# Even frequencies of a split DFT: two quarter-size units in place of two half-size units (FNet mixing and gated convolution FFN, one core)

## The chip, the cores and the metric

The kernel runs on one core of a Trainium2 chip. The metric is the device time of one execution in microseconds (us). A core has five engines that run side by side: PE (TensorE, matmuls; its weight loads are listed as PEld), DVE (VectorE), ACT (ScalarE), POOL (GpSimd) and SP, which issues most DMAs. SBUF is the working memory; matmuls write to PSUM, which holds banks of 512 fp32 numbers in each of 128 partitions.

## The reference

```
X = np.fft.fft(x, axis=1)                 # x: (8, 3136, 256), over the sequence
X = np.fft.fft(X, axis=2)                 # over the features
x1 = X.real
h = np.maximum(x1 @ w_in, 0.0)            # w_in: (256, 1024)
conv_out = sum over k of conv_w[k] * (h shifted by k - 1 rows)    # 3 taps, zero padded
out = (h * sigmoid(conv_out)) @ w_out     # w_out: (1024, 256)
```

All of it is fp32. A matmul in fp32 stands in the trace as two records, each with a weight load of its own.

## The kernel before, in words

**Sequence DFT by halves.** The DFT over 3136 rows is taken of folded data: rows n, S-n, S/2-n and so on are added or subtracted on DVE (`fold_ops`), so that a quarter of the rows (784) stays, in tiles `w` of 98 or 99 partitions, for even and for odd frequencies apart. For one batch and one of the two sums, `sn` = 0 (cosine, tile `pt`) or 1 (sine, tile `qt`), the values at the frequencies k = 0 to 1568 are made by products of these tiles with tables of cosines and sines (`product`, line 273; `table`, line 216). The sum over n goes over four groups q = 0 to 3 (n mod 4 decides the group; 98 or 99 rows each).

A split halves the columns: with the groups q = 3 and 1 summed to a number a, and q = 2 and 0 to a number b, frequency k is a + b, and its mirror image M - k is a - b (or b - a for the sine). So a product is made only for half of the frequencies, and one addition and one subtraction give the rest.

- **Odd k** (`odd_even`, line 308, and `odd`, line 323) are made with one more level of it. `odd_even` makes the groups q = 1 and q = 3 for 196 columns each; ACT copies one half to a tile `as`, and DVE's addition and subtraction (lines 318 and 320) put 392 numbers into another tile `as`. `odd` then makes the groups 0 and 2 for 392 columns, and DVE combines the `as` tile with them into `pt` or `qt` at every second place (lines 330 and 332).
- **Even k** (`even(sn, c)`, line 286) are made by two units, one for c = 0 and one for c = 1: the frequencies 0, 4, 8, ... (197 columns) and 2, 6, 10, ... (196 columns). Each unit has four matmuls of 197 or 196 columns: q = 3 and 1 accumulate in the first part of a PSUM bank, q = 2 and 0 in the part behind it. The columns of the table are read with a step of 2, the PSUM output is contiguous. ACT copies the first part to `as` (line 295), then DVE adds and subtracts straight into `pt` or `qt` at every fourth place (lines 299 and 302).

**Order of the work.** The rest of the kernel goes in 256 steps (8 batches x 4 chunks of the sequence x 8 groups of 128 features of d_ff). In cycle t of the loop PE runs `products` of step t+1 (matmuls into `pb` and `pa`: the feature DFT merged with `w_in`), `mm2` of step t-3 (six matmuls `po` with `wout`), and, last, matmuls of a DFT unit, which all write to `pd` (one PSUM bank of a pool with one buffer). DVE runs `combine` (line 692), two taps of the convolution (line 702), one piece of side work between the taps, and its half of the gate (line 723). ACT copies `pb` (683), fills `pa` (662), does the first tap (697), the sigmoid (715) and the copies of the output (742); POOL does the other half of the gate (722, 725) and issues indirect loads of x (131).

The eight units of batch b run during the loop cycles of batch b-1: `cs` (line 857 on) gives each of them n // 8 cycles. For b = 2 to 7 that is four cycles, one matmul in each; for b = 1 it is one or two cycles, four or two matmuls in each, in nine cycles together. A unit's ACT copy and its DVE part (`u.copy` and `u.fin`, lines 861 and 862) stand in the cycle after its last matmul. Batch 0's units run ahead of the loop (line 786), in `po` buffers, with no steps beside them. The first matmul of the next unit waits until the DVE part of the one before has read `pd`.

Of the kernel before, what the change touches and what calls it, by code (L numbers as in the profile page):

```python
# [9 lines left out]
F32 = mybir.dt.float32  # L10
# [3 lines left out]
ALU = mybir.AluOpType  # L14
# [22 lines left out]
def kernel(  # L37
# [10 lines left out]
    nc = tc.nc  # L48
    B, S, D = x.shape
    F = moe_w_in.shape[1]  # L50
    P = 128
    M = S // 2
    Q4 = S // 4
# [4 lines left out]
    HE = Q4 // 2 + 1  # L58
    HO = Q4 // 2
# [14 lines left out]
    asp = ctx.enter_context(tc.tile_pool(name="asp", bufs=4))  # L74
# [11 lines left out]
    vt = nc.vector.tensor_tensor  # L86
# [4 lines left out]
    def mm(o, l, r, start, stop):  # L91
        nc.tensor.matmul(o, l, r, start=start, stop=stop, skip_group_check=True)  # L92
# [120 lines left out]
    PQ, eb, er = {}, {}, {}  # L213
    ed = edp.tile([B, (RC // 2 + 1) * RC], F32, name="ed")

    def table(k, st, q, cols):
        return tabs[st // 2][0:k, st, q, cols] if st < 2 else tabs[1][0:k, st - 2, q, cols]
# [32 lines left out]
    class Unit:  # L250
# [19 lines left out]
        def fin(self):  # L270
            self.fin_(self.p)

    def product(o, w, st, q, cols, start, stop):

        def f(p):
            k = KR if q == HQ - 1 else NP
            mm(p[o], w(k, q), table(k, st, q, cols), start, stop)
        return f

    def units(b):  # L280
        def w(i):
            return lambda k, q: wt[b][i // 4][0:k, i % 4, q, :]

        a_ = {}

        def even(sn, c):
            n = HO // 2 + 1 - c
            nh = HO // 2
            cols = slice(c, HE, 2)
            mms = [product((slice(0, P), slice(j * n, (j + 1) * n)), w(2 * sn + c), sn, q, cols, q == qs[0], q == qs[1])  # L290
                   for j, qs in enumerate(((3, 1), (2, 0))) for q in qs]

            def copy(p):
                a_[sn, c] = asp.tile([P, HO + 2], F32, name="as", tag="as")
                nc.scalar.copy(out=a_[sn, c][:, 0:n], in_=p[:, 0:n])

            def fin(p):
                a, bb, t = a_[sn, c], p[:, n:2 * n], PQ[b][sn]
                vt(t[:, 2 * c:Q4 + 1:4], a[:, 0:n], bb, op=ALU.add)
                hi = t[:, M - 2 * c:Q4:-4]  # L300
                x0, x1 = (bb[:, 0:nh], a[:, 0:nh]) if sn else (a[:, 0:nh], bb[:, 0:nh])
                vt(hi, x0, x1, op=ALU.subtract)
            return Unit(b, mms, copy, fin)

        def stat(sn):
            return ((w(4 + 2 * sn), 2 + sn), (w(5 + 2 * sn), 4 + sn))

        def odd_even(sn):
            mms = [product((slice(0, P), slice(j * QO, (j + 1) * QO)), wf, st, q, slice(0, QO), i == 0, i == 1)
                   for j, q in ((1, 1), (0, 3)) for i, (wf, st) in enumerate(stat(sn))]  # L310

            def copy(p):
                a_[sn], a_["e0"] = [asp.tile([P, HO + 2], F32, name="as", tag="as") for _ in range(2)]
                nc.scalar.copy(out=a_["e0"][:, 0:QO], in_=p[:, 0:QO])

            def fin(p):
                a, e0, e2 = a_[sn], a_["e0"][:, 0:QO], p[:, QO:2 * QO]
                vt(a[:, 0:QO], e0, e2, op=ALU.add)
                x0, x1 = (e2, e0) if sn else (e0, e2)
                vt(a[:, HO - 1:QO - 1:-1], x0, x1, op=ALU.subtract)  # L320
            return Unit(b, mms, copy, fin)

        def odd(sn):
            prods = [(q, wf, st) for q in (0, 2) for wf, st in stat(sn)]
            mms = [product((slice(0, P), slice(0, HO)), wf, st, q, slice(0, HO), i == 0, i == 3)
                   for i, (q, wf, st) in enumerate(prods)]

            def fin(p):
                a, bb, t = a_[sn][:, 0:HO], p[:, 0:HO], PQ[b][sn]
                vt(t[:, 1:Q4 + 1:2], a, bb, op=ALU.add)  # L330
                x0, x1 = (bb, a) if sn else (a, bb)
                vt(t[:, M - 1:Q4:-2], x0, x1, op=ALU.subtract)
            return Unit(b, mms, lambda p: None, fin)

        def feature():

            mms = []
            for i in range(2):
                for j, qs in enumerate(((3, 1), (2, 0))):
                    for c in range(2):  # L340
                        n = HO // 2 + 1 - c
                        o = 32 * (2 * j + c)
                        mms.append(product((slice(o, o + 1), slice(0, n)),
                                           lambda k, q, c=c: ea[b][0:k, c, q:q + 1], 0, qs[i],
                                           slice(c, HE, 2), i == 0, i == 1))

            def copy(p):
                a_["e"] = [asp.tile([P, HO + 2], F32, name="as", tag="as") for _ in range(2)]
                for j in range(2):
                    for c in range(2):  # L350
                        n = HO // 2 + 1 - c
                        o = 32 * (2 * j + c)
                        nc.scalar.copy(out=a_["e"][c][0:1, j * n:(j + 1) * n], in_=p[o:o + 1, 0:n])

            def fin(p):
                t = er[b]
                nh = HO // 2
                for c in range(2):
                    n = nh + 1 - c
                    a, bb = a_["e"][c][0:1, 0:n], a_["e"][c][0:1, n:2 * n]  # L360
                    gt(t[:, 2 * c:Q4 + 1:4], a, bb, op=ALU.add)
                    gt(t[:, M - 2 * c:Q4:-4], a[:, 0:nh], bb[:, 0:nh], op=ALU.subtract)
            return Unit(b, mms, copy, fin, True)

        def begin():
            PQ[b] = [pqp.tile([P, NK], F32, name=nm, tag=nm) for nm in ("pt", "qt")]

        def row():
            er[b] = erp.tile([1, NK], F32, name="er", tag="er")
            nc.sync.dma_start(out=er[b], in_=PQ[b][1][P - 1:P, :])  # L370

        def flip():

            act(er[b][:, 3:NK:4], er[b][:, 3:NK:4], AF.Copy, scale=-1.0)

        def store():
            nc.sync.dma_start(out=ed[b:b + 1, 0:NK], in_=er[b])

        return (begin, [odd_even(1), odd(1), even(1, 0), even(1, 1), feature(), odd_even(0), odd(0),
                        even(0, 0), even(0, 1)], row, flip, store)  # L380

    class Feature:

# [368 lines left out]
    def keep_on(banks):  # L752

        for p in banks:
            mm(p.rearrange("p (s q d) -> p s q d", s=2, q=2), wt[0][1][0:NP, 1, 0], wt[0][1][0:NP, 0:2, 0:2],
               True, True)

    begin, us, row, flip, store = units(0)
    begin()

# [34 lines left out]
    n = chunks[0].k1  # L795
    p = psd.tile([P, 512], F32, name="pd", tag="pd")
# [54 lines left out]
    for b in range(1, B):  # L851
        begin, us, *_ = units(b)
        us = us[0:4] + us[5:]
        c0, n = ends[b], per * b - 3 - ends[b]
        at(max(c0, per * (b - 1) + 1), "pe", begin)
        cs = [c0 + i * n // len(us) for i in range(len(us) + 1)]
        for i, u in enumerate(us):
            k = cs[i + 1] - cs[i]
            for j in range(k):
                at(cs[i] + j, "pe", lambda u=u, j=j, k=k: u.matmuls(j, k))  # L860
            at(cs[i + 1], "act", u.copy)
            at(cs[i + 1], "dve", u.fin)
            if b > 1:
                taken.add(cs[i + 1])
        at(cs[-1] - 2, "load", lambda b=b: spread(b, range(len(chunks) - 1)))
        at(per * b + 1, "load", lambda b=b: spread(b, [len(chunks) - 1]))
    for b in range(1, B):
        ops, singles = fold_ops(b)
        c0, n = ends[b - 1], ends[b] - ends[b - 1]
# [14 lines left out]
    n = len(steps)  # L884
# [101 lines left out]
```

## Time and profile before

| | |
|---|---|
| median of three runs | 1202.16 us (1201.81 to 1203.91) |
| the profiled execution's own time | 1202.16 us |
| span of that execution, from its first to its last instruction | 1200.4 us |
| units of batch 0 for even k on PE | 34.28 to 40.09 us |
| units of batch 1 on PE | 149.7 to about 196 us |
| units of batches 2 to 7 on PE | from 233 to about 1049 us |
| granted TensorE clock, mean | 0.997 |

Busy time of an engine counts the time in which at least one of its instructions was in flight. In the views by line a group stands as: line, engine, operation, output tile <- input tiles, shapes, count, then busy time and mean ns of one instruction, then idle time ahead of it and what ended it. A timeline line gives start, length, engine, line, operation, tiles, shapes (for matmuls rows*columns of the weights, then partitions x columns that stream) and count; matmuls overlap, so what one costs is the distance from its start to the next start, not its length. The chain of waits follows the work that ended last back from the end.

### The profile page before, as it was taken

What the parts mean: (1) busy time and instruction counts of PE and PEld (TensorE: products, weight loads), DVE (VectorE), ACT (ScalarE), POOL (GpSimd) and SP (SyncE); (2) the same over time, 40 slices, a digit from 0 to 9 for tenths busy, and PEclk for the clock granted to TensorE, in tenths of its full rate; (3) what the DMA queues carried; (4) which work ended last, traced back from release to release, by engine and by line L of the source; (5) the groups of instructions that cost most, each with busy time, mean ns of one, the idle gap of its engine ahead of it and who ended that gap; (6) DMA issues with size and microseconds to landing.
All of it is one profiled execution on the core that took longest, in us unless ns stands there. A gap on an engine that the chain in (4) does not pass through costs nothing.

```text
span 1200.4 us, 15341 instructions
## 1 busy us (share of the span) xinstructions
PE 1162.4 (97%) x4802; PEld 895.6 (75%) x4802; DVE 1130.0 (94%) x1642; ACT 883.4 (74%) x1840; POOL 474.2 (40%) x540
## 2 busy tenths in 40 slices
PE   4978999999999999999999999999999999999998
PEld 2756677677777777777777777777777777777776
DVE  7899999999999999999999999999998988899996
ACT  2667656777677777777777777787776777788884
POOL 5325636464263432624345243632334223342224
PEclk9999999999999999999999999999999999999999
DMA  9712243212031210202021020310000100110000
GB/s 230 187 34 81 58 53 101 62 54 74 8 95 45 67 40 30 79 27 81 26 89 51 17 64 27 95 40 27 27 27 28 32 27 27 47 34 27 27 28 31
DMA packets 70068, 66.08 MB, mean 55 GB/s; under 512 B 28107, under 2 KB 57683, under 8 KB 69987
## 3 DMA queue, kind: packets, MB, share of 16 engines
q1 hardware_dynamic: 64349, 51.98, 15.3%
q0 software_dynamic: 5120, 12.85, 3.5%
q8 instruction: 38, 0.62, 0.2%
q14 instruction: 43, 0.35, 0.1%
q10 hardware_dynamic: 518, 0.28, 0.1%
HBM read 39.33 MB, written 25.74 MB: 54 GB/s over the span
## 4 chain that ended last, share of the span: by engine, by line
PE 83%; DVE 7%; issue 4%; POOL 3%; ACT 2%; DMA 1%; ACTq 0%; POOLq 0%; DVEq 0%; SPq 0%
PE po L92 50%; PE pb L92 13%; PE pa L92 12%; PE pd L92 8%; DVE g L702 3%; POOL xh L131 1%; DVE h L692 1%; DVE g L723 1%; DMA xh<-in_x_dram 1%; ACT nb L683 1%; ACT g L715 0%; POOL left L725 0%; ACT os L742 0%; POOL g L722 0%; DVE w L194 0%
## 5 line engine op out<-in xcount | busy, mean ns | idle before, releaser
L92 PE MATMUL po<-wout,g 128*128 128x256 f32 x3072 | 708.6, 380 | 15.9 <-DVE g L723 15.7
L92 PEld LDWEIGHTS po<-wout,g 128*128 128x128 f32 x3072 | 581.5, 190 | 163.8 <-DVE g L723 30.4
L702 DVE SCALAR_TENSOR_TENSOR g<-h,cw,g 128x770 f32<-128x770 f32 (+1 forms) x512 | 573.1, 1119 | 6.0 <-ACT g L697 2.1
L722 POOL TENSOR_TENSOR g<-g,h 128x385 f32<-128x385 f32 (+1 forms) x256 | 271.5, 1061 | 681.3 <-ACT g L715 482.6
L683 ACT ACTIVATE nb<-pb 128x386 f32<-128x386 f32 (+3 forms) x512 | 227.2, 498 | 168.2 <-PE pb L92 167.6
L715 ACT ACTIVATE g<-g 128x385 f32<-128x385 f32 (+2 forms) x512 | 244.4, 529 | 101.4 <-DVE g L702 99.6
L692 DVE CUSTOM_DVE_ANT_0 h<-pa,nb 128x386 f32<-128x386 f32 (+3 forms) x512 | 264.3, 556 | 6.5 <-POOL h L668 6.5
L697 ACT ACTIVATE g<-h,cw 128x770 f32<-128x770 f32 (+1 forms) x256 | 244.0, 953 | 0.0
L92 PE MATMUL pb<-qt,G 127*128 127x387 f32 (+2 forms) x512 | 212.7, 496 | 1.4 <-ACT G L631 1.0
L92 PE MATMUL pa<-pt,G 128*128 128x387 f32 (+2 forms) x512 | 211.8, 494 | 0.0
L662 ACT ACTIVATE pa<-eb,ge 128x387 f32<-128x387 f32 (+2 forms) x256 | 154.5, 604 | 2.7 <-DVE h L692 1.9
L92 PEld LDWEIGHTS pa<-pt,G 128*128 128x128 f32 x512 | 96.8, 189 | 73.6 <-issue 18.2
L723 DVE TENSOR_TENSOR g<-g,h 128x385 f32<-128x385 f32 (+1 forms) x256 | 146.4, 572 | 2.2 <-ACT g L715 2.2
L92 PE MATMUL pd<-tab,w 98*128 98x196 f32 (+3 forms) x448 | 126.7, 374 | 0.0
L131 POOL DMA_INDIRECT xh<-in_x_dram,idx x64 | 107.6, 1681 | 13.3 <-issue 10.6
L92 PEld LDWEIGHTS pb<-qt,G 127*128 127x128 f32 x512 | 93.9, 190 | 19.5 <-issue 1.6
L92 PEld LDWEIGHTS pd<-tab,w 98*128 98x128 f32 (+1 forms) x448 | 84.7, 191 | 12.3
L725 POOL TENSOR_TENSOR left<-g,h 128x64 f32<-128x64 f32 x64 | 64.8, 1012 | 0.0
L742 ACT COPY os<-po 128x256 f32<-128x256 f32 x196 | 57.5, 390 | 8.0 <-PE po L92 4.7
L156 DVE TENSOR_TENSOR xh<-xh 98x1020 f32<-98x1020 f32 (+1 forms) x32 | 39.5, 1239 | 2.3 <-DMA xh<-in_x_dram,idx 2.3
L167 DVE TENSOR_TENSOR xh<-xh 98x1024 f32<-98x1024 f32 (+1 forms) x32 | 38.9, 1217 | 0.1
L193 DVE TENSOR_TENSOR w<-xh 98x508 f32<-98x508 f32 (+1 forms) x32 | 22.8, 714 | 0.2
(114 smaller groups left out, 324.9 us busy)
## 6 DMA issues: line engine op xcount, KB each, us to landing
out_dram<-os SPq DMA_DIRECT2D x192, 128.0 KB
xh<-in_x_dram SPq DMA_DIRECT2D x16, 784.0 KB
eb<-ed SPq DMA_DIRECT2D x16, 193.5 KB
tab<-dft_seq_dram SPq DMA_DIRECT2D x4, 589.5 KB
raw<-in_moe_w_in_dram SPq DMA_DIRECT2D x4, 512.0 KB
raw<-in_moe_w_out_dram SPq DMA_DIRECT2D x1, 2048.0 KB
eb<-ed SPq DMA_DIRECT2D x8, 209.0 KB
eb<-ed SPq DMA_DIRECT2D x7, 193.0 KB
```

The costliest lines, as they stand in the source:

```text
L92: nc.tensor.matmul(o, l, r, start=start, stop=stop, skip_group_check=True)
L131: nc.gpsimd.indirect_dma_start(out=xh[b, h][0:NP, 7 - m].rearrange("p q d -> p (q d)"), out_offset=None, in_=bass.AP(tensor=x.tensor, offs ...
L662: act(pa[s][:, 0:n], eb[b, c], AF.Copy, scale=ge[:, f:f + 1])
L683: act(nb[s][:, i, cols], p[:, cols], AF.Copy, scale=-1.0 if i else 1.0)
L692: nc.vector._custom_dve(TENSOR_ADD_SAT, out=to, in0=a[:, cols], in1=c[:, i, cols], s0=BIG, s1=0.0)
L697: act(gs[s], hs[s][:, 0:n], AF.Copy, scale=cw[:, 0, s[2]:s[2] + 1])
L702: stt(out=g, in0=h[:, k:k + n], scalar=cw[:, k, f:f + 1], in1=g, op0=ALU.mult, op1=ALU.add)
L715: act(gs[s][:, c], gs[s][:, c], AF.Sigmoid)
L722: gt(g[:, p], g[:, p], h[:, p], op=ALU.mult)
L723: vt(g[:, v], g[:, v], h[:, v], op=ALU.mult)
L725: gt(left[:, f, b % 2 * LEFT:(b % 2 + 1) * LEFT], g[:, r], h[:, r], op=ALU.mult)
L742: nc.scalar.copy(out=osb[:, j % 2], in_=pt[:, j % 2])
```

## The change

For even k, the two units by c become two units by q, as for odd k:

- `even_even(sn)` takes q = 3 and 1 for the first n = 197 columns alone. It has four matmuls, each by itself (start and stop), of 99 or 98 columns: c = 0 and c = 1 of q = 3 to the even and odd places of the first part of the bank, c = 0 and c = 1 of q = 1 to those of the second part. ACT copies the first part (197 columns) to an `as` tile, and DVE's addition and subtraction write 197 and 196 numbers contiguously to another `as` tile.
- `even(sn)` takes q = 2 and 0 for all 393 columns: four matmuls, c = 0 (197 columns, to the even places of the bank) and c = 1 (196 columns, to the odd places), two accumulating on each. It has no ACT copy. DVE's addition (393 numbers) and subtraction (392) write to `pt` or `qt` at every second place.

The number of units, of matmuls, of weight loads and of DVE instructions stays; PSUM outputs that were contiguous have a step of 2 now. The number of `as` tiles taken stays as well.

```diff
-        def even(sn, c):
-            n = HO // 2 + 1 - c
-            nh = HO // 2
-            cols = slice(c, HE, 2)
-            mms = [product((slice(0, P), slice(j * n, (j + 1) * n)), w(2 * sn + c), sn, q, cols, q == qs[0], q == qs[1])
-                   for j, qs in enumerate(((3, 1), (2, 0))) for q in qs]
+        def even_even(sn):
+
+            n = HO // 2 + 1
+            mms = [product((slice(0, P), slice(j * n + c, (j + 1) * n, 2)), w(2 * sn + c), sn, q, slice(c, n, 2),
+                           True, True) for j, q in ((0, 3), (1, 1)) for c in range(2)]
 
             def copy(p):
-                a_[sn, c] = asp.tile([P, HO + 2], F32, name="as", tag="as")
-                nc.scalar.copy(out=a_[sn, c][:, 0:n], in_=p[:, 0:n])
+                a_["v", sn], a_["e4"] = [asp.tile([P, HO + 2], F32, name="as", tag="as") for _ in range(2)]
+                nc.scalar.copy(out=a_["e4"][:, 0:n], in_=p[:, 0:n])
 
             def fin(p):
-                a, bb, t = a_[sn, c], p[:, n:2 * n], PQ[b][sn]
-                vt(t[:, 2 * c:Q4 + 1:4], a[:, 0:n], bb, op=ALU.add)
-                hi = t[:, M - 2 * c:Q4:-4]
-                x0, x1 = (bb[:, 0:nh], a[:, 0:nh]) if sn else (a[:, 0:nh], bb[:, 0:nh])
-                vt(hi, x0, x1, op=ALU.subtract)
+                a, e4, e2 = a_["v", sn], a_["e4"], p[:, n:2 * n]
+                vt(a[:, 0:n], e4[:, 0:n], e2, op=ALU.add)
+                x0, x1 = (e2[:, 0:n - 1], e4[:, 0:n - 1])[::1 if sn else -1]
+                vt(a[:, HO:n - 1:-1], x0, x1, op=ALU.subtract)
             return Unit(b, mms, copy, fin)
+
+        def even(sn):
+
+            mms = [product((slice(0, P), slice(c, HE, 2)), w(2 * sn + c), sn, q, slice(c, HE, 2), q == 2, q == 0)
+                   for c in range(2) for q in (2, 0)]
+
+            def fin(p):
+                a, bb, t = a_["v", sn][:, 0:HE], p[:, 0:HE], PQ[b][sn]
+                vt(t[:, 0:Q4 + 1:2], a, bb, op=ALU.add)
+                x0, x1 = (bb, a) if sn else (a, bb)
+                vt(t[:, M:Q4:-2], x0[:, 0:HO], x1[:, 0:HO], op=ALU.subtract)
+            return Unit(b, mms, lambda p: None, fin)
...
-        return (begin, [odd_even(1), odd(1), even(1, 0), even(1, 1), feature(), odd_even(0), odd(0),
-                        even(0, 0), even(0, 1)], row, flip, store)
+        return (begin, [odd_even(1), odd(1), even_even(1), even(1), feature(), odd_even(0), odd(0),
+                        even_even(0), even(0)], row, flip, store)
```

## The prediction

> **What bounds the kernel now.** I read the page first, by engine and by the chain of waits:
>
> ```profile
> PE 1162.4 (97%) x4802; PEld 895.6 (75%) x4802; DVE 1130.0 (94%) x1642; ACT 883.4 (74%) x1840; POOL 474.2 (40%) x540
> PE 83%; DVE 7%; issue 4%; POOL 3%; ACT 2%; DMA 1%; ACTq 0%; POOLq 0%; DVEq 0%; SPq 0%
> ```
>
> PE and DVE both look full, so the share of busy time does not decide; the chain does, and it runs on PE for 83% of the span. Then the busy times of stretches (after each stretch: length, PE, PEld, DVE, ACT, POOL, clock, DMA):
>
> ```profile
> 150.00:200.00 50.00, 50.00 (x210) 38.85 (x210) 48.17 (x76) 32.13 (x66) 22.96 (x23) 1.00 0.44 84
> 240.00:381.00 141.00, 141.00 (x586) 109.98 (x585) 134.38 (x201) 105.57 (x218) 66.14 (x70) 1.00 0.18 58
> 522.00:663.00 141.00, 141.00 (x588) 110.31 (x587) 134.50 (x197) 107.00 (x220) 57.00 (x64) 1.00 0.17 53
> ```
>
> From 240 us on PE is never without a matmul in flight, and all units of batches 2 to 7 lie there or just ahead. That a busy PE also runs at its pace needs start distances, since lengths overlap. The timeline of PE gives them:
>
> ```profile
> 527.87 0.51 PE L92 MATMUL pd<-tab,w 98*128 98x197 f32 x2
> 528.23 0.81 PE L92 MATMUL pb<-qt,G 127*128 127x387 f32 x2
> 528.88 0.82 PE L92 MATMUL pa<-pt,G 128*128 128x387 f32 x2
> 529.53 2.75 PE L92 MATMUL po<-wout,g 128*128 128x256 f32 x12
> 532.12 0.52 PE L92 MATMUL pd<-tab,w 98*128 98x197 f32 x2
> ```
>
> One cycle is 4.25 us: pd 0.36, pb 0.65, pa 0.65, po 2.59. Nothing is left between the pieces. So PE's own work sets the pace here, and a nanosecond taken from `pd` is a nanosecond of the time, as long as DVE, ACT and POOL keep up.
>
> **The change on PE.** Columns first. For one sum of one batch, before: four matmuls of 197 and four of 196, 1572 columns. After: two of 99, two of 98, two of 197, two of 196, 1180. The matmuls and their weight loads stay eight. So the question is what a matmul of 98 or 99 columns costs. The nearest rows, of 197 columns (above), 196 columns read contiguously, and one column, all with weights of 128 columns:
>
> ```profile
> 561.85 0.50 PE L92 MATMUL pd<-tab,w 98*128 98x196 f32 x2
> 562.18 0.81 PE L92 MATMUL pb<-qt,G 127*128 127x387 f32 x2
> ...
> 45.75 0.95 PE L92 MATMUL po<-dm,win 128*128 128x1 f32 x8
> 46.56 0.90 PE L92 MATMUL pb<-qt,G 127*128 127x386 f32 x2
> 47.29 0.81 PE L92 MATMUL pa<-pt,G 128*128 128x386 f32 x2
> ```
>
> 196 columns cost 0.33 us for the pair of records, 197 columns with a step of 2 in the table 0.36 (0.348 to 0.360 over the loop's even units; I use 0.355). One column costs far more than nothing: eight records take 45.75 to 46.56 = 0.81, and the pb behind them takes 0.73 to its pa in place of 0.65, so 0.89 / 8 = 0.111 per record. That is the weight load, which can't be outrun: 0.222 per matmul. By columns alone 99 would cost half of 0.355 = 0.178. The larger one holds: 0.222. A matmul of `even_even` saves 0.355 - 0.222 = 0.133 us; bounds are 0.177 saved (if only columns counted) and a loss of 0.025 (if the load, 0.190 long in its rows, did not overlap at all and set 0.38). I take 0.133, since the one-column row is the same load at the same pace.
>
> `even` keeps matmuls of 197 and 196 columns with the same step in the table: saving 0, if writing to PSUM with a step of 2 costs nothing. No matmul of before writes with a step, so this is the unknown. From below: nothing, since columns, weights and reads are the same (a gain has no source). From above: as if it walked over the skipped columns too, which is a matmul of 392 columns, 0.661 in place of 0.355 (574.54 to 575.20 on the timeline). Between them: reading with the step costs 0.355 against 0.335, 6%; and DVE, writing 196 numbers at every fourth place, takes 0.35 where contiguous ones take 0.28 (chain rows below), 25%. I take 0, as PE's own row with a step is nearest, and even that is nearly free; I keep 0.02 (6%) for my range.
>
> The rule that speaks against the change: the Trainium skill, "PSUM — Partial Sum Buffer", section Specifications, says that PSUM lines hold 8 bytes, two fp32, and that a non-contiguous access pattern slows matmuls significantly. It gives no factor. No run here shows it; if the factor were two (an estimate of mine from "two per line"), `even` would lose what the change gains, and more: the sum would be that of the first rival below. The reason why I do not follow it: an fp32 matmul streams a column in 0.85 ns (0.335 / 2 / 196), and the page does not say at which pace its line rule was seen.
>
> Per batch: 8 matmuls of `even_even` (4 for each sum) x 0.133 = 1.06 us less on PE.
>
> **The change on DVE and ACT.** The chain of waits shows DVE's pace without idle time, ahead of the loop:
>
> ```profile
> 33.57 0.27 DVE as L318
> 33.84 0.28 DVE as L320
> ...
> 34.77 0.47 DVE pt L332
> ...
> 40.92 0.35 DVE qt L299
> 41.27 0.36 DVE qt L302
> ```
>
> Before, four instructions at every fourth place: 4 x 0.35 = 1.42 per sum. After, two like L318 and two like L332: 2 x 0.275 + 2 x 0.48 = 1.51. So DVE gets 0.09 more per sum, 0.18 per batch, of about 134 busy in 141. ACT loses one copy of 0.33 per sum. With it goes a wait: the tile `as` rows give 26.2 us of DVE's idle time in 26 waits to ACT's copies of line 295, 1.0 us each; half of the units had their copy removed, so DVE gets back up to 14 x 1.0 in the loop, against 7 x 0.18 = 1.3 more work. What `even`'s DVE part then waits for is PE itself, whose matmul ended the cycle before; line 330 in the same place waits 0.9 us in 14. DVE stays covered by PE: of a stretch of 141 it had about 6.6 idle.
>
> The `pd` bank is free for the next unit when `even`'s two DVE instructions end: 0.96 in place of 0.71 after their start, which comes up to 1.0 earlier. No new wait.
>
> **Where the gain arrives.** Against the profiled execution (time 1202.16, span 1200.4; its time is also the median):
>
> - Batches 2 to 7: 6 x 1.06 = 6.4. Nothing follows the loop but PE's own end, so it stays.
> - Two places in these batches where PE did wait, 0.3 us each, at 497.9 and 779.9 for DVE's gate, at the end of a run of fold instructions. There up to four faster matmuls (0.5) lie ahead, so PE will wait longer; DVE's removed wait pays part back. I take 0.2 lost at each: -0.4.
> - Batch 1, units at 150 to 196 with PE full; from 187 to 211 the chain goes over ACT and POOL, then DVE. What PE gains until 187 moves that start; DVE-bound stretches may take some. Between 0.5 and 1.06: 0.8.
> - Batch 0: PE saves 1.06, but the chain from 40.07 to 47 is DVE's, which takes 0.18 longer, behind narrowing of weights that ends at 40.15 as before. PE's saving is hidden: -0.2.
>
> Sum: 6.4 - 0.4 + 0.8 - 0.2 = 6.6 us less. 1202.16 - 6.6 = **1195.6 us**. With 6% on each stepped write (8 x 0.02 x 7 = 1.1) and 1 us of the gain lost to waits, 1197.7; with `even_even` at its columns' price (8 x 0.044 x 7 = 2.5 more) 1193.1. Own range of this case: 1193.5 to 1198.
>
> **Rivals.**
>
> 1. *The stepped write sets the pace: slower.* One mechanism, in PE on `even`'s matmuls. At its upper price `even` goes from 0.355 to 0.661, 8 x 0.306 = 2.45 more per batch, and `even_even` to about 0.335, saving 0.02 x 8 = 0.16. Net 2.3 per batch, all on the bounding engine in seven batches: +16, **1218 us**. It decides from where `even` loses what `even_even` gains, 0.133 of 0.355: a stepped column 37% dearer. For it: DVE's stepped write shows that such a price exists. Against it: the stepped read costs PE 6%.
> 2. *Partial price, or a weight load that costs more: no change.* With DVE's 25% as the price, `even` loses 0.09 a matmul, and 8 x (0.133 - 0.09) = 0.35 per batch is left: 2.4 in seven batches, less the 0.6 of waits: **1200.4**. With the load not overlapped, +0.2 per batch: 1203.6.
> 3. *DVE takes over.* If PE's gain turns into waits for DVE's gate in half of the batches, as it did twice before, 3.3 is left: **1198.9**. DVE's removed waits speak against it. It is still faster.
>
> **Chances.** Forecast 0.66; DVE takes over 0.09; no change (2) 0.12; slower (1) 0.13. What a measurement of this kernel can tell from no change is about 0.2%, 2.4 us. Faster by more: 0.66 + 0.09 = 0.75, plus nothing from (2): 0.75. Same 0.12, slower 0.13. The range runs from 1193.5 over (3) to the better part of (2), 1202: it leaves out (1), 0.13, and the tails, 0.06.
>
> **What would show it.** `pd` matmuls of 98 and 99 columns with start distances of 0.11 (0.22 the pair): right; 0.17 or more: weight load mis-sized. `pd` of 197 columns at 0.355: stepped write free; at 0.38 to 0.66: the rivals. The group of line 295's successor with 14 copies in the loop and half the idle time ahead of DVE; PE busy in all of 240 to 1190 as before. Were PE's idle time for the gate to grow beyond 2 us, the third rival is there. The prediction is wrong above all if the stepped write has a price above a third.

## The result and the profile after

The changed kernel takes 1196.78 us (median of 4 runs, 1195.33 to 1197.23), the kernel before 1203.04 (median of 4, 1201.81 to 1204.11) in the same sessions: a ratio of 0.9946, 95% interval 0.9929 to 0.9963. It is faster, by 6.3 us. (Against 1202.16, the median that the forecast started from, it is 5.4.) The profiled execution of the changed kernel has a span of 1195.3 us against 1200.4. From `odd_even` on (the former line 308) the lines of the code are ten higher (L702, L712, L733 are the former L692, L702, L723); `even_even` copies in L294 and combines in L298 and L300, `even` combines in L310 and L312.

The page's lines of engine busy time and of the chain by engine:

```profile
PE 1156.0 (97%) x4802; PEld 888.5 (74%) x4802; DVE 1135.0 (95%) x1642; ACT 878.4 (73%) x1824; POOL 477.5 (40%) x540
PE 86%; DVE 5%; issue 3%; POOL 3%; ACT 2%; DMA 0%; ACTq 0%; POOLq 0%; DVEq 0%; SPq 0%
```

PE lost 6.4 us of busy time, ACT 5.0 with its 16 copies, and the chain lies on PE even more than before. The same stretches as in the prediction:

```profile
150.00:200.00 50.00, 50.00 (x216) 39.07 (x217) 49.19 (x77) 33.95 (x69) 24.05 (x27) 1.00 0.42 82
240.00:381.00 141.00, 141.00 (x589) 109.48 (x589) 136.29 (x203) 106.23 (x218) 68.84 (x70) 1.00 0.19 58
522.00:663.00 141.00, 141.00 (x591) 110.00 (x591) 136.20 (x199) 106.94 (x222) 57.04 (x64) 1.00 0.17 53
```

PE is never without a matmul from 240 us on (before, it had two pauses there, of 0.17 and 0.16), and does more of them in each stretch (591 in place of 588 in the last one). PE's timeline shows at what pace:

```profile
527.22 0.36 PE L92 MATMUL pd<-tab,w 99*128 99x98 f32 x2
527.42 0.84 PE L92 MATMUL pb<-qt,G 127*128 127x387 f32 x2
528.10 0.82 PE L92 MATMUL pa<-pt,G 128*128 128x387 f32 x2
528.75 2.75 PE L92 MATMUL po<-wout,g 128*128 128x256 f32 x12
...
539.59 0.52 PE L92 MATMUL pd<-tab,w 98*128 98x197 f32 x2
539.94 0.81 PE L92 MATMUL pb<-qt,G 127*128 127x387 f32 x2
```

Read the start distances. The pair of 98 columns takes 0.20 to the next start; the pb behind it takes 0.68 to its pa where it took 0.65. The cheaper pair leaves a debt of 0.02: the first record takes 0.093, the second 0.111, which is what a weight load took in the one-column row, and 0.347 in place of 0.328 pass between pb's two records (mean over the 22 places with 387 columns). I read that as loads that run late. Together 0.224, the price of two weight loads. The pair of 197 columns, whose output now has a step of 2, takes 0.354, as it did with a contiguous output.

On DVE's side, the groups by the tiles `as` (durations min/median/max) and the waits for ACT's copies:

```profile
L298 DVE TENSOR_TENSOR as<-as,pd x14: 360/361/362, 167.3 to 1027.7; 128x197 f32<-128x197 f32 x14
L310 DVE TENSOR_TENSOR qt<-as,pd x7: 552/558/569, 172.4 to 973.9; 128x393 f32<-128x393 f32 x7
...
  ACT as L324: 12.5, 10
  ACT as L294: 9.8, 13
```

DVE waits 22.3 us for the copies where it waited 26.2 + 8.5 = 34.7; `even` waits for none.

**Where the time went.** I split the span at the first matmul of `po<-wout,g` (the loop's start) and at the same matmul of batch 7, and take the batch periods between, from the starts in the traces (batches count from 0; the units of batch b run in the period of batch b-1). All runs but one, which adds work behind the loop, in us:

| run | loop start | from there to batch 7 | period of batch 2 | period of batch 3 | median of the runs |
|---|---|---|---|---|---|
| before | 60.84 | 1012.09 | 139.52 | 142.54 | 1202.2 to 1203.0 |
| after | 63.75 | 1004.12 | 138.04 | 141.51 | 1196.78 |
| after_again | 63.06 | 1004.13 | 138.04 | 141.51 | 1196.52 |
| pe_undone | 62.00 | 1011.29 | 139.08 | 142.53 | 1202.71 |
| pe_alone | 64.27 | 1004.89 | 138.48 | 141.49 | 1197.64 |
| old_b0 | 63.18 | 1004.12 | 138.04 | 141.51 | 1195.96 |
| flat_write | 62.40 | 1004.10 | 138.04 | 141.51 | 1196.12 |
| flat_tables | 62.77 | 1003.18 | 137.90 | 141.36 | 1195.18 |
| fill | 61.13 | 1004.31 | 138.04 | 141.51 | 1195.23 |
| before_fill | 61.28 | 1012.10 | 139.51 | 142.53 | 1202.47 |
| fill_flat_tables | 61.51 | 1003.22 | 137.90 | 141.36 | 1194.02 |

The loop gained 7.97 us. The start gave 2.9 of them back in the profiled execution: 7.97 - 2.90 = 5.07, the spans differ by 5.1. Two questions follow: which part of the change carries the loop's gain, and whether the start's loss belongs to the change.

### The profile page after: what moved, and what is told of

The parts are those of the page before. It is cut to its first block, busy times and chain, and to the rows that moved or that the text cites. A ratio compares the mean times of both kernels' runs of the same rounds, so it can differ in the third digit from the quotient of the medians.

```text
span 1195.3 us, 15307 instructions
## 1 busy us (share of the span) xinstructions
PE 1156.0 (97%) x4802; PEld 888.5 (74%) x4802; DVE 1135.0 (95%) x1642; ACT 878.4 (73%) x1824; POOL 477.5 (40%) x540
## 4 chain that ended last, share of the span: by engine, by line
PE 86%; DVE 5%; issue 3%; POOL 3%; ACT 2%; DMA 0%; ACTq 0%; POOLq 0%; DVEq 0%; SPq 0%
PE po L92 53%; PE pb L92 13%; PE pa L92 13%; PE pd L92 7%; DVE g L712 2%; POOL xh L131 1%; DVE h L702 1%; DVE g L733 1%; ACT nb L693 0%; ACT os L752 0%; ACT g L725 0%; POOL left L735 0%; POOL g L732 0%; DVE w L194 0%; ACT pa L672 0%
## 5 line engine op out<-in xcount | busy, mean ns | idle before, releaser
L712 DVE SCALAR_TENSOR_TENSOR g<-h,cw,g 128x770 f32<-128x770 f32 (+1 forms) x512 | 580.1, 1133 | 6.2 <-ACT g L707 2.2
L732 POOL TENSOR_TENSOR g<-g,h 128x385 f32<-128x385 f32 (+1 forms) x256 | 276.2, 1079 | 673.0 <-ACT g L725 471.1
L702 DVE CUSTOM_DVE_ANT_0 h<-pa,nb 128x386 f32<-128x386 f32 (+3 forms) x512 | 264.1, 556 | 7.4 <-POOL h L678 6.5
L733 DVE TENSOR_TENSOR g<-g,h 128x385 f32<-128x385 f32 (+1 forms) x256 | 147.4, 576 | 2.2 <-ACT g L725 2.2
L92 PE MATMUL pd<-tab,w 98*128 98x196 f32 (+3 forms) x448 | 118.4, 356 | 0.0
L92 PEld LDWEIGHTS pb<-qt,G 127*128 127x128 f32 x512 | 91.2, 190 | 19.3 <-ACT G L641 2.0
L178 POOL COPY w<-xh 98x4 f32<-98x4 f32 (+1 forms) x32 | 20.6, 644 | 6.1 <-DVE xh L167 3.6
```

Source lines behind the costliest of these rows:

```text
L702: nc.vector._custom_dve(TENSOR_ADD_SAT, out=to, in0=a[:, cols], in1=c[:, i, cols], s0=BIG, s1=0.0)
L712: stt(out=g, in0=h[:, k:k + n], scalar=cw[:, k, f:f + 1], in1=g, op0=ALU.mult, op1=ALU.add)
L732: gt(g[:, p], g[:, p], h[:, p], op=ALU.mult)
L733: vt(g[:, v], g[:, v], h[:, v], op=ALU.mult)
```

## Experiments

My theory for the loop: PE's own work sets the pace, and PE's saving carries the gain. The rival: the removed ACT copies and their waits carry it. For the start, two theories: DVE's longer units, or PE's clock.

**after_again** is the changed kernel once more, with no edit.

> The changed kernel once more, unaltered. Both theories of the gain: 1196 to 1197.5 us. It tells about the start: in the first profile of the changed kernel the first matmul of the loop with wout began at 63.7 us in place of 60.8. If the change itself delays the start (the two DVE units, 0.4 us longer, let PE run idle), 63 to 64 us again; if the half clock there, at 41.6 to 48.4 us, is chance, about 61 us.

Measured: 1196.52 us (ratio 0.9951, 0.9937 to 0.9964), loop start 63.06. So the late start came again, with half clock at 42.8 to 46.2 us.

**pe_undone** gives `even_even` its old number of columns:

```diff
-            mms = [product((slice(0, P), slice(j * n + c, (j + 1) * n, 2)), w(2 * sn + c), sn, q, slice(c, n, 2),
+            mms = [product((slice(0, P), slice(j * n, (j + 1) * n - c)), w(2 * sn + c), sn, q, slice(c, HE, 2),
```

> The changed kernel with DVE's and ACT's part as changed, but even_even's four matmuls have 197 or 196 columns again (contiguous output, other table columns, so the even frequencies come out as other sums). Theory PE: the loop's batches 1 to 7 lose their 1.04 us each again, 7.2 in all: 1203.5 to 1204.5 us, batch periods at 142.5 in place of 141.5. Rival, the removed ACT copies and their waits carry the gain: the time stays at 1196 to 1198 us.

Measured: 1202.71 us, ratio 1.0000 (0.9991 to 1.0009). The whole gain is gone, and the periods are 1.01 to 1.04 longer than in the changed kernel: PE's columns carry it. But the loop is 0.80 shorter than before (in its profile a later start, 62.00, hides that), by batches 2 and 4, whose periods lost 0.44 each. There DVE was what PE waited for. Before, and then in this run:

```profile
496.87 0.81 PE L92 MATMUL pb<-qt,G 127*128 127x386 f32 x2
497.52 0.81 PE L92 MATMUL pa<-pt,G 128*128 128x386 f32 x2
498.50 0.70 PE L92 MATMUL po<-wout,g 128*128 128x256 f32 x2 [0.17 <-DVE g L723]
```

```profile
497.79 0.50 PE L92 MATMUL pd<-tab,w 99*128 99x196 f32 x2
498.12 0.81 PE L92 MATMUL pb<-qt,G 127*128 127x386 f32 x2
498.77 0.81 PE L92 MATMUL pa<-pt,G 128*128 128x386 f32 x2
499.42 2.75 PE L92 MATMUL po<-wout,g 128*128 128x256 f32 x12
```

pa to po is 0.65 here, a matmul's own time, in place of 0.98 before; the other 0.11 of the 0.44 lies between the first two matmuls of `po`. With DVE's and ACT's part as changed, the wait of PE is gone. Which piece of that part does it (the removed copies, or DVE's other instructions) was not tried apart.

**pe_alone** takes the other half: the kernel before, with the matmuls of `even(sn, 0)` cut, DVE and ACT as they were.

```diff
+            def some(j, i, q):
+                cut = (0, HO // 4 + 1, n)
+                o, e = (cut[i], cut[i + 1]) if c == 0 else (0, n)
+                return product((slice(0, P), slice(j * n + o, j * n + e)), w(2 * sn + c), sn, q,
+                               slice(c + 2 * o, c + 2 * e - 1, 2), i == 0 or c == 0, i == 1 or c == 0)
+            mms = [some(j, i, q) for j, qs in enumerate(((3, 1), (2, 0))) for i, q in enumerate(qs)]
```

> The kernel before, with only PE's saving: the four matmuls of the unit even(sn, 0) have 99 or 98 columns, each alone writes its part of the bank; DVE and ACT as before (so q = 3 and 1 are not summed there and these frequencies come out as other values). No stepped PSUM output. Theory PE: 7 x 1.04 = 7.3 less in the loop, nothing changed ahead of it: 1195.5 to 1197 us, and PE waits at the two places before batch ends (497.9 and 779.9 before) grow from 0.3 to 0.6 us, since DVE is not relieved. Rival (DVE and ACT carry it): 1202 to 1203 us.

Measured: 1197.64 us (0.9961, 0.9947 to 0.9974), with a late start (64.27). The loop is 7.20 shorter than before: 7 x 1.03. The same place in its timeline:

```profile
497.92 0.81 PE L92 MATMUL pa<-pt,G 128*128 128x386 f32 x2
498.90 1.78 PE L92 MATMUL po<-wout,g 128*128 128x256 f32 x7 [0.17 <-DVE g L726]
```

The wait is there, 0.98 from pa to po, and has not grown, as I had expected it to. So the two parts add up: 7.20 from PE, 0.80 from DVE and ACT, 7.97 in the changed kernel.

**old_b0** keeps the kernel before for batch 0, whose units run ahead of the loop.

```diff
+        e1, e0 = [[even_c(s, 0), even_c(s, 1)] if b == 0 else [even_even(s), even(s)] for s in (1, 0)]
+        return (begin, [odd_even(1), odd(1), *e1, feature(), odd_even(0), odd(0), *e0], row, flip, store)
...
```

(`even_c` is `even(sn, c)` of the kernel before.)

> The changed kernel, but batch 0, ahead of the loop, keeps the two units by c of the kernel before; batches 1 to 7 are as changed. If the change delays the start by 2.9 us: 1193.5 to 1194.5 us, loop start at 60.8. If the delay is chance or the clock's: 1196 to 1197 us, within 0.3 of the changed kernel in the same call.

Measured: 1195.96 us (0.9947, 0.9933 to 0.9960), loop start 63.18, with half clock at 43.1 to 46.5. The old units did not bring the early start back, and the half clock came with them too. So DVE's longer units are not needed for a late start; the clock came into question. The stretches 41.6 to 48.4 us (PE, PEld, DVE, ACT, POOL, then the clock) of before and of the first profile after:

```profile
41.60:48.40 6.80, 6.34 (x32) 4.64 (x32) 6.56 (x16) 3.93 (x10) 3.29 (x6) 1.00 0.62 206
```

```profile
41.60:48.40 6.80, 6.34 (x18) 4.64 (x18) 6.46 (x14) 1.90 (x5) 2.83 (x6) 0.50 0.67 212
```

PE is as busy, with 18 matmuls for 32, at a clock of 0.50. PE's timeline there, before and then in the changed kernel:

```profile
40.09 0.91 PE L92 MATMUL pd<-er,one 1*128 1x386 f32 x2
41.02 1.02 PE L92 MATMUL po<-dm,win 128*128 128x1 f32 x8
41.91 1.97 PE L92 MATMUL po<-win,dm 128*128 128x256 f32 x8
44.34 0.92 PE L92 MATMUL pb<-qt,G 127*128 127x386 f32 x2 [0.46 <-issue]
```

```profile
39.66 0.91 PE L92 MATMUL pd<-er,one 1*128 1x386 f32 x2
41.40 1.64 PE L92 MATMUL po<-dm,win 128*128 128x1 f32 x8 [0.82 <-ACT eb L809]
42.90 3.76 PE L92 MATMUL po<-win,dm 128*128 128x256 f32 x8
47.12 1.55 PE L92 MATMUL pb<-qt,G 127*128 127x386 f32 x2 [0.46 <-ACT G L641]
```

PE has finished its shorter units at 39.73, 1 us ahead of DVE, whose narrowing of weights ends at 40.75 (before, both ended at about 40.15). It sits idle for 0.82 between matmuls of one row (`pd<-er,one`) and matmuls of one column (`po<-dm,win`). Then the eight matmuls of `po<-win,dm`, 1.97 long before, take 3.76, and the loop's first products come 2.8 later.

**fill** takes that stretch away: a dense matmul in the gap, and the one-column matmuls (`column(0)`) behind the eight matmuls `po<-win,dm` (`blocks(0)`).

```diff
-    column(0)
+    keep_on([idle])
     for f in load_ops(1, 0, nc.sync):
         f()
     blocks(0)
+    column(0)
```

> The changed kernel with another order of PE at 40 to 48 us: one dense matmul of 512 columns (into the idle bank) where PE sat idle for 1 us behind the product with 'one', and column(0), eight records of one column, behind blocks(0) in place of ahead of it. Theory clock: in the changed kernel PE reaches this place 1 us sooner than DVE and is idle there, 2.6 to 2.9 us of little work in a row, and the clock falls to half for 3.4 to 6.8 us, which delays the loop by 2 to 3 us in most executions. With no such stretch left the clock stays at 1.0 there, the loop starts at 60.5 to 61.5 us, and the median falls to 1193.5 to 1194.5. Rival (the delay is DVE's 0.4 us longer work and late loads): loop start at 63, 1196 to 1197 us.

Measured: 1195.23 us (0.9937, 0.9925 to 0.9950), loop start 61.13, clock 1.0 throughout this part:

```profile
38.80 0.91 PE L92 MATMUL pd<-er,one 1*128 1x386 f32 x2
39.64 1.12 PE L92 MATMUL pb<-w 98*128 98x512 f32 x2
40.60 2.22 PE L92 MATMUL po<-win,dm 128*128 128x256 f32 x8
42.66 0.95 PE L92 MATMUL po<-dm,win 128*128 128x1 f32 x8
43.47 0.89 PE L92 MATMUL pb<-qt,G 127*128 127x386 f32 x2
```

The loop start is where it was expected; the median fell by 1.3 against after_again, not by the 2 to 3 I expected, and by 0.9 against flat_write below (1196.12), which was measured beside it and has the changed kernel's order of PE. The intervals of these runs overlap, so the times by themselves do not show the gain; the profile shows the clock and the start.

**before_fill** makes the same edit in the kernel before.

> The kernel before with the same new order of PE at 40 to 48 us. Theory clock: the kernel before falls to half clock in fewer executions, so it gains less, 0.5 to 1.5 us: 1200.8 to 1201.8. The distance to the run fill is then the loop's alone, 7.5 to 8.2 us, larger than the 5.7 to 6.3 between the two kernels as they are. Rival (no effect of the clock): 1202 to 1203, and a distance of 6.

Measured: 1202.47 us (0.9995, 0.9986 to 1.0004): no gain that can be told. The distance to fill is 7.24, near the loop's 7.8 between these two (1012.10 - 1004.31). So with the start out of the way the change is worth some 1 us more than the medians of the two kernels as they are show, by the medians; the intervals leave room for none. What did go is the upper end: before_fill's eleven executions end at 1202.72, while 9 of the 17 of the kernel before beside them took longer, up to 1204.78.

How firm is the clock's part? Of the 12 profiles, six show PE idle behind the product with `one`, 0.5 to 1.0 us long (after, after_again, pe_alone, flat_write, flat_tables, step_bench): all six have half clock there. Six show no gap at that point (before, pe_undone, old_b0, before_fill, fill, and fill_flat_tables, which idles 0.40 ahead of that product): one of them, old_b0, has it. So the gap makes it likely and is not needed for it; old_b0's program is that of before up to the loop, so the moment at which the activity is judged plays a part. All half clocks at this place last 3.4 or 6.8 us.

The traces' clock records show that moment. Within one run the half clocks begin at whole multiples of 3.413 us from each other (after_again: 42.81 and 114.49, 21 times; flat_tables: 42.58, 69.88 and 114.26, 8 and 21 times), so the grid of windows can be laid over the stretch ahead. In the seven runs with half clock, the window that ends where it begins holds 0.5 to 1.6 us of matmuls of more than one row and one column (from start to start). old_b0's holds 1.59, with 1.80 of matmuls of one row or one column and 0.02 idle. In the five others no window from 36 to 47 us holds less than 1.97. So here it is the share of such matmuls in a window that goes with the half clock, and where the grid falls; the gap is one way to lower it. Where the line lies is not shown: at other places windows with 1.5 to 1.6 us passed at full clock. The Trainium skill, "TensorE: Matmul & The Clock Gate", Part 1, says that the clock gate judges PE's activity in free-running windows of 3.4 us and halves the clock after an idle one: the length and the free run agree with the multiples. But no window here was idle as a whole.

How much of the late start is the clock's? The first matmul of batch 0's units (`po<-tab,w`) itself moves, from 24.67 to 26.09 us in these profiles; why was not examined. From it to the loop's start it takes 35.91 and 36.05 us with DVE's old units at full clock (before, before_fill), 36.12 to 36.46 with the new ones at full clock (pe_undone, fill, fill_flat_tables), 37.00 to 37.13 with 3.4 us of half clock (old_b0 with its old units among them), and 38.18 and 38.22 with 6.8. So 3.4 us of half clock cost 0.5 to 1.2 us, 6.8 cost 1.7 to 2.3, DVE's new units 0.1 to 0.5, and of the 2.9 and 2.2 lost in after and after_again 0.6 and 1.1 lie ahead of the units.

**flat_write** makes every PSUM output of the new units contiguous, to try the disputed step.

```diff
+            def to(j, c):
+                m = n // 2 + 1
+                return slice(j * n + c * m, j * n + (n if c else m))
+            mms = [product((slice(0, P), to(j, c)), w(2 * sn + c), sn, q, slice(c, n, 2),
...
+            mms = [product((slice(0, P), slice(c * m, HE if c else m)), w(2 * sn + c), sn, q, slice(c, HE, 2), q == 2, q == 0)
...
```

> The changed kernel, but each matmul of even_even and even writes a contiguous part of the bank (even places in front, odd ones behind), and DVE reads as before, so the even frequencies come out in another order. If the step of 2 in PSUM is free at fp32's pace, as the 0.354 of the first profile says: pairs at 0.354 and 0.204, batch periods at 141.51 and 138.04 as in the changed kernel, 1196 to 1197 us. If it has a price that is hidden so far: shorter pairs in even, up to 1 us less.

Measured: 1196.12 us (0.9946, 0.9933 to 0.9959); loop length 1004.10 against 1004.12, pairs of `even` and `even_even` 0.354 and 0.206 (means over the whole loop, as in the changed kernel). The step in PSUM costs nothing here.

**step_bench** measures the step by itself, behind the last step of the loop.

```diff
+    half16 = gp.tile([P, HW - 2], F32, name="h16", tag="g")[:, 0:192].bitcast(mybir.dt.bfloat16)
+    nc.vector.tensor_copy(half16, wout[:, 0:2].rearrange("p f d -> p (f d)")[:, 0:384])
+    p = psd.tile([P, 512], F32, name="bench", tag="pd")
+    for l, r in ((half16[:, 0:P], half16[:, P:P + D]), (wout[:, 0, 0:P], wout[:, 1])):
+        for step in (1, 2, 1, 2):
+            for _ in range(12):
+                mm(p[:, 0:(D - 1) * step + 1:step], l, r, True, True)
```

> The changed kernel with 96 matmuls behind its last step, all into one unused bank, 256 columns each: 12 with contiguous output, 12 with a step of 2 in PSUM, the same again, first in bf16 (one record each), then in fp32 (two records each). It measures the disputed cost of the step by itself; its time is longer by the added work. If the step is free at fp32's pace only because fp32 streams a column at half the pace of bf16: fp32 0.216 per record for both outputs, bf16 about 0.109 contiguous and 0.2 or more with the step. If the step is free at any pace: 0.109 for both bf16 groups. If it costs fp32 something that the short units hid: more than 0.22 per stepped fp32 record.

Measured, on PE's timeline (first twelve bf16 matmuls contiguous, then twelve with the step; then 23 fp32 records of the contiguous group, and 23 of the stepped one):

```profile
1189.77 1.47 PE L92 MATMUL bench<-h 128*128 128x256 bf16 x12
1191.08 2.75 PE L92 MATMUL bench<-h 128*128 128x256 bf16 x12
...
1197.79 5.13 PE L92 MATMUL bench<-wout 128*128 128x256 f32 x23
...
1202.96 5.13 PE L92 MATMUL bench<-wout 128*128 128x256 f32 x23
```

bf16 goes from 0.109 from start to start to 0.216 with the step; fp32 stays at 0.216 with and without. The step costs a factor of two at bf16's pace, and nothing at fp32's, which is half of it. (The first of the stepped bf16 matmuls is 0.174 ahead of the second, the others 0.216.)

**flat_tables** sorts the columns of the even table (even places in front) as it is made on the way in (M0 = 197), so that no unit for even k reads with a step; the table's other readers are adapted to it.

```diff
-        k = 2 * np.arange(QN // 2 + 1) + par
+        i = np.arange(QN // 2 + 1)
+        k = 2 * (i if par else np.concatenate([i[::2], i[1::2]])) + par
...
-            mms = [product((slice(0, P), slice(j * n + c, (j + 1) * n, 2)), w(2 * sn + c), sn, q, slice(c, n, 2),
+            mms = [product((slice(0, P), slice(j * n + c, (j + 1) * n, 2)), w(2 * sn + c), sn, q, slice(c * M0, c * M0 + M0 // 2 + 1 - c),
                            True, True) for j, q in ((0, 3), (1, 1)) for c in range(2)]
...
-            mms = [product((slice(0, P), slice(c, HE, 2)), w(2 * sn + c), sn, q, slice(c, HE, 2), q == 2, q == 0)
+            mms = [product((slice(0, P), slice(c, HE, 2)), w(2 * sn + c), sn, q, slice(c * M0, HE if c else M0), q == 2, q == 0)
```

> The changed kernel with the even table's columns sorted on the way in (even places in front, odd ones behind), so that no matmul of the units for even k reads with a step; the PSUM outputs keep theirs, and the result is the reference's. If the step in reading is what makes 0.354 of 0.335, and the pair of even_even is bound by its weight loads: even's pairs 0.335, even_even's with the matmul behind it 0.224 as before; 8 x 0.019 = 0.15 per batch, 1.1 us in seven batches: 1195 to 1196 us, periods at 141.36. If even_even were bound by its columns, it would fall as well, to 0.17, and the sum would be 2.5 us.

Measured: 1195.18 us (0.9934, 0.9922 to 0.9946); loop length 1003.18, 0.94 less than the changed kernel (1.1 expected), periods 0.14 to 0.15 shorter. `even`'s pair is at 0.336, as its timeline shows (538.25 to 538.59):

```profile
538.25 0.50 PE L93 MATMUL pd<-tab,w 98*128 98x197 f32 x2
538.59 0.82 PE L93 MATMUL pb<-qt,G 127*128 127x387 f32 x2
```

`even_even`'s pair went from 0.206 to 0.202, but the pb behind it gave 0.005 back (0.352 between its records): the two weight loads still cost 0.22. That pair is bound by its loads, not by its columns.

**fill_flat_tables** joins the last two edits that gained.

> The changed kernel with both alterations that gained: the order of PE at 40 to 48 us of the run fill, and the sorted even table of the run flat_tables. If the two are independent: loop start at 61 us, batch periods 141.36, 1195.2 less 1.1, so 1193.8 to 1194.5 us, with a spread as small as in fill. If the start's delay is only moved, 1195 to 1196.

Measured: 1194.02 us (0.9929, 0.9915 to 0.9943), loop start 61.51, periods 141.36. By the medians it beats both kernels, by 8.6 us and about 2.5 (the latter across sessions). The spread, 2.2 us, is larger than fill's 1.5, against what I expected.

## Why the prediction was right, and what in it was not

The time (1196.78 against 1195.6 forecast, 6.3 less against 6.6) is right, and the main mechanism is shown. That the sum fits so well is partly luck: two of its small terms were wrong on opposite sides (the waits gave 0.9 where I took 0.4 off, the start took 2.9 in the profile where I took 0.2), and the fourth execution of the kernel before moved its median 0.9 above the 1202.16 that I subtracted from.

- **PE's price of `even_even`: right.** 0.222 forecast, 0.224 measured with the debt that it leaves to pb. 8 x 0.133 = 1.06 per batch; pe_alone shows 1.03.
- **The stepped PSUM output: right, and now shown.** Free in the kernel (flat_write) and by itself (step_bench). The page that I weighed, "PSUM — Partial Sum Buffer", Specifications, is right at bf16's pace (0.109 to 0.216) and does not hold at fp32's; it names no pace. My estimate of a factor of two fits bf16. The first rival's condition is not met.
- **Batches 2 to 7, the two places where PE waited: wrong.** I took 0.2 off at each because PE would come earlier to a DVE that is late. The waits vanished instead, +0.44 each, and with that they had cost more than the 0.3 I read. In pe_alone, with the faster matmuls alone, the wait stayed as it was, as if DVE's lateness there followed PE's pace (that link was not tried by itself). And pe_undone shows that DVE's and ACT's part of the change takes the wait away. I had named the removed wait for ACT's copy as what pays back, and booked it too low, if it is that piece.
- **Batch 1: near.** 0.8 forecast, 0.94 measured (batch 0's period, 165.39 to 164.45).
- **The start: wrong.** I booked 0.2 lost to DVE's 0.18 longer work, and that part measured 0.1 to 0.5. The profiled executions lost 2.2 to 2.9, by the half clock (0.5 to 2.3 us) and by a later start of batch 0's units, which no edit here tried. PE's saving was not only hidden: with it PE's windows there hold fewer matmuls, and the clock fell in all six profiles that have the saving and the old order of PE for batch 0, and in one of four without the saving. old_b0 shows that the old start can fall into it too. Single executions tell a little of how often: of 41 of the kernel before in the sessions of the experiments, 11 have a mean clock of 0.996 and take 1202.7 to 1204.8, the 30 others 1201.1 to 1203.5; of nine of the changed kernel, eight have 0.996 or 0.997, and the one at 0.998 took 1193.5. Where in these the clock fell is not recorded.
- **DVE's work and the third rival.** DVE's waits for copies fell by 12.4 us (14 forecast), and PE did not wait for DVE more in the loop. DVE's busy time gained 5 us (forecast 1.4). By the pages the taps of the convolution, the same 512 instructions, went from 573.1 to 580.1 us; why was not tried. It had no effect on the loop.

The sum as measured in the profiles: 7.20 from PE, 0.80 from DVE and ACT (7.97 together in the changed kernel), -2.9 at the start. What stays open is 0.6 between the 7.2 of fill against before_fill and the 7.8 of their loops, which is within their intervals.

## What to carry to other kernels

Price a short matmul by the larger of its columns and its weight load, and look at the matmul behind it for the rest of the bill. Where an engine is made faster ahead of a point at which it waits, ask what its new idleness, and the thin matmuls beside it, do to its own clock; a dense matmul in the gap, or another order, kept the clock full here. Compare two starts from a common event close ahead, since what lies ahead of it moves too. Price a wait that is removed at the very places where the bounding engine waits, rather than on average.

## What the runs showed of the hardware that I had not expected

- An output step of 2 in PSUM doubles a bf16 matmul (0.109 to 0.216 us for 256 columns) and leaves an fp32 one at 0.216.
- A step of 2 in the streamed SBUF operand costs an fp32 matmul 5 to 6% (pairs of 0.354 against 0.336), while the same step in PSUM costs nothing.
- PE fell to half clock for 3.4 to 6.8 us, at multiples of 3.413 us within a run, after windows of that length with 0.5 to 1.6 us of matmuls of more than one row and one column, without a longer pause (0.02 to 1.0 us idle).
